# Head sums of half the sequence as accumulating transfers in place of matmuls, with 1 KB weight rows, four open output tiles and an early gate

## Chip, cores, metric

The kernel runs on one core of one Trainium2 chip. The metric is the device time of one execution in microseconds. Executions of one kernel mostly agree within 1%; each run below is four executions (one of them profiled) unless said otherwise, beside executions of the kernel before on the same chip.

## The reference, cut to what matters

Input x is 2048 x 512, everything bfloat16. The output mixes two branches with a gate per row.

```python
g = sigmoid((x * gate_w).sum(-1))                       # one number per row
# branch A: 32 heads of 16, each row attends to 8 rows, 0, 2, ..., 14 back
logits = einsum("bhsd,bhswd->bhsw", q, kg) * scale      # head sums: over d = 16
attn   = softmax(where(mask, logits, -1e9))
a      = einsum("bhsw,bhswd->bhsd", attn, vg) @ wo
# branch B: an MLP over the sequence axis
u = gelu(einsum("bsd,sf->bdf", layernorm(x), w1) + b1)  # f = 1792
y = einsum("bdf,fs->bds", u, w2) + b2
out = g * a + (1 - g) * y.transpose
```

## The kernel before: the parts that matter

The kernel is written as a list of operations with what each reads and writes; a small list scheduler in the kernel file orders them on each engine. `A("dve", ...)` puts one operation on an engine, `sch.dma("pool", ...)` issues a transfer from GpSimd (POOL). The sequence is treated in two halves `h`. TensorE (PE) does all matmuls; the vector engine (DVE) does the attention's products. Cuts are marked `# ...`.

```python
def f_sum(h, b0, with_gate):            # head sums on PE: 16 matmuls, 32 columns wide each
    # ... the 16 gate matmuls first if with_gate
        for wp in range(4):
            for c in range(4):
                ins = e.matmul(ps[32*c:32*c+32, 4+wp, :], lhsT=RP, rhs=sub(PB[b0], ...), tile_position=(0, 32*c))

for h in range(2):
    # ... q*k products of half h on DVE, in six buffers of 1 MB
    A("pe", f_sum(h, b0, h == 0), ..., name="sum%d" % h)
    A("act", act(LOG[h], ps[:, 4:8, :], AF.Copy), ..., name="lev%d" % h)     # logits leave PSUM
    A("dve", tt(M4, LOG[h][:, 0:4, :], LOG[h][:, 4:8, :], ALU.max), ...)     # softmax begins
    # ... max, subtract, exp, sums, 1/sum
    A("dve", tt(ATT[h], ATT[h], ..., ALU.mult), ..., name="nrm%d" % h)       # normalised weights
    for c in range(4):                  # spread them over the partitions: four copies of 512 KB
        prev = sch.dma("pool", ... e.dma_start(d_, s_) ..., name="av%d_%d" % (h, c))

AVD = (3, 4, 5)                         # attention products of 8 tiles; first add of these by DMA
def av_mult(u):
    AV(tt(pv, V5..., AVW[h]..., ALU.mult), 4.4, name="avm%d" % u)
    if u in AVD:
        sch.dma("pool", ... e.dma_start(o_, i_, accum_op=ALU.add) ..., name="avd%d" % u)   # 1 MB
def av_add4(u):
    if u not in AVD:
        AV(tt(pw(0, 4), pw(0, 4), pw(4, 4), ALU.add), 2.25, name="ava%d" % u)
def av_add(u):                          # two small adds, then the output projection may run
    AV(...1.19, name="avb%d" % u); AV(tt(OT[:, u], ...), 0.66, name="avc%d" % u)
```

Tile `u` needs copy `u % 4` of its half; the fifth product (`avm4`) is the first that needs a copy of half two. The three tiles whose big add is a transfer (3, 4, 5) are finished two products later.

## Time and profile before

| | before |
|---|---|
| time, median (range) | 165.43 us (165.14 to 165.48) |
| span of the profiled execution | 163.0 us |
| PE, DVE busy | 97%, 93% |
| softmax weights of half two normalised | 112.4 us |
| first of their copies issued; last landed | 112.70; 128.20 |
| first accumulating add issued; landed | 126.29; 134.11 |
| PE's last matmul ends | 159.54 |

How to read it: PE is busy nearly all of the span, so PE's own work sets the time, and DVE is close behind.

### The profile page before, as it was taken

The numbers are of one execution on the slowest core, as the hardware profiler recorded it, in microseconds if no ns is written. First come the engines' busy times: TensorE is split into PE (matmuls) and PEld (weight loads), VectorE is DVE, ScalarE is ACT, GpSimd is POOL, SyncE is SP. The second block draws the span as 40 slices with busy tenths as digits, with TensorE's granted clock in tenths as the row PEclk, the third lists the DMA queues.
The fourth block names the chain that finished last, engine by engine and source line by source line (L and its number), as shares of the span: only waits on it lengthen the run. The fifth ranks groups of instructions, "written<-read, shape, count | busy, mean of one in ns | idle before, by whom it ended". The sixth has DMA issues, their size and how long they took to land.

```text
span 163.0 us, 1989 instructions
## 1 busy us (share of the span) xinstructions
PE 158.6 (97%) x793; PEld 77.2 (47%) x808; DVE 151.1 (93%) x126; ACT 70.2 (43%) x100; POOL 12.0 (7%) x36
## 2 busy tenths in 40 slices
PE   7999999999999999999999999999999999999993
PEld 4855555555544344444444344444444444444641
DVE  1789999999999999999999999999999999999961
ACT  3367677666771579662111348011111111111164
POOL 3000030020000000023000000003100222000000
PEclk9999999999999999999999999999999999999999
DMA  5999979729499095999998976981997899991014
GB/s 165 311 268 259 221 183 263 140 38 191 101 277 292 24 242 157 261 290 290 303 245 233 260 188 177 290 209 30 300 243 193 186 207 193 205 216 36 32 59 134
DMA packets 44685, 32.24 MB, mean 198 GB/s; under 512 B 7941, under 2 KB 42245, under 8 KB 44677
## 3 DMA queue, kind: packets, MB, share of 16 engines
q1 hardware_dynamic: 41444, 22.06, 51.6%
q0 software_dynamic: 2512, 9.44, 27.3%
q10 hardware_dynamic: 720, 0.62, 1.2%
q8 instruction: 6, 0.10, 0.2%
q14 instruction: 3, 0.02, 0.0%
HBM read 18.88 MB, written 2.10 MB: 129 GB/s over the span
## 4 chain that ended last, share of the span: by engine, by line
PE 97%; ACT 1%; issue 1%
PE ps L858 30%; PE ps L885 30%; PE ps L649 23%; PE ps L894 8%; PE ps L588 2%; PE ps L551 2%; PE ps L722 1%; ACT arena L453 1%; PE ps L717 1%; PE ps L567 1%; PE ps L604 0%
## 5 line engine op out<-in xcount | busy, mean ns | idle before, releaser
L450 DVE TENSOR_TENSOR arena<-arena 128x4096 bf16<-128x4096 bf16 (+8 forms) x79 | 131.9, 1718 | 1.6 <-ACT arena L453 0.6
L885 PE MATMUL ps<-arena 128*128 128x512 bf16 (+2 forms) x234 | 50.0, 366 | 0.2
L858 PE MATMUL ps<-arena 128*128 128x512 bf16 x218 | 48.5, 379 | 0.3
L453 ACT ACTIVATE arena<-ps,arena 128x512 bf16<-128x512 f32 (+1 forms) x30 | 21.8, 731 | 60.7 <-PE ps L894 37.7
L453 ACT ACTIVATE arena<-ps 128x512 bf16<-128x512 f32 (+3 forms) x53 | 32.9, 629 | 17.4 <-PE ps L649 10.9
L649 PE MATMUL ps<-arena 128*128 128x512 bf16 x173 | 38.0, 379 | 0.2
L885 PEld LDWEIGHTS ps<-arena 128*128 128x128 bf16 x238 | 22.8, 98 | 25.9
L858 PEld LDWEIGHTS ps<-arena 128*128 128x128 bf16 x224 | 21.7, 98 | 26.8 <-issue 0.8
L649 PEld LDWEIGHTS ps<-arena 128*128 128x128 bf16 x176 | 19.9, 113 | 18.0
L894 PE MATMUL ps<-arena 128*128 128x512 bf16 (+2 forms) x67 | 15.6, 366 | 0.1
L453 ACT ACTIVATE arena<-arena 128x16 f32<-128x16 f32 (+5 forms) x10 | 6.7, 678 | 9.7 <-DVE arena L450 9.6
L954 ACT ACT_TABLE_LOAD x7 | 9.0, 1283 | 2.8 <-issue 2.7
L894 PEld LDWEIGHTS ps<-arena 128*128 128x128 bf16 x68 | 6.5, 98 | 7.3
L692 DVE BATCH_NORM_STATS2 arena<-arena 128x6 f32<-128x512 bf16 x16 | 9.9, 679 | 0.1
L790 POOL DMA_DIRECT2D arena<-arena x8 | 4.3, 560 | 75.1 <-DVE arena L450 75.1
L706 DVE TENSOR_SCALAR arena<-arena 128x512 bf16<-128x512 bf16 x16 | 5.3, 404 | 0.0
L827 POOL DMA_DIRECT2D arena<-arena x3 | 3.6, 1209 | 17.7 <-DVE arena L450 17.7
L747 POOL DMA_DIRECT2D arena<-arena x2 | 2.5, 1268 | 30.6 <-DVE arena L692 20.2
L579 DVE CAST arena<-ps 128x256 bf16<-128x256 f32 x4 | 1.6, 422 | 3.2 <-PE ps L567 3.2
L588 PE MATMUL ps<-arena 128*128 128x256 bf16 (+1 forms) x27 | 3.8, 284 | 0.2 <-ACT arena L453 0.2
L551 PE MATMUL ps<-const-bfloat16-1.0 128*128 128x512 bf16 (+1 forms) x9 | 2.7, 483 | 0.8 <-PEq L1004 0.8
L588 PEld LDWEIGHTS ps<-arena 128*128 128x128 bf16 x28 | 2.9, 113 | 0.7 <-DVE arena L579 0.4
(30 smaller groups left out, 14.4 us busy)
## 6 DMA issues: line engine op xcount, KB each, us to landing
arena<-in_B_w_dram SPq DMA_DIRECT2D x7, 1024.0 KB, 6.8
arena<-in_B_w_dram SPq DMA_DIRECT2D x8, 896.0 KB, 9.4
arena<-arena POOLq DMA_DIRECT2D x5, 1024.0 KB, 9.7
arena<-arena POOLq DMA_DIRECT2D x8, 512.0 KB, 11.2
out_dram<-arena SPq DMA_DIRECT2D x15, 128.0 KB, 3.1
arena<-in_A_x_dram SPq DMA_DIRECT2D x3, 512.0 KB, 4.7
arena<-in_A_wqkv_dram SPq DMA_DIRECT2D x2, 256.0 KB, 3.8
arena<-in_A_wqkv_dram SPq DMA_DIRECT2D x1, 512.0 KB, 5.6
```

Of the source, the lines that this page charges most:

```text
L450: return lambda e: e.tensor_tensor(out=o_, in0=a_, in1=b_, op=op_)
L453: return lambda e: e.activation(out=o_, in_=i_, func=f_, **kw)
L551: ins = e.matmul(ps[:, 7, 0:n_], lhsT=C1, rhs=nc.const_aps.tensor(1.0, (128, n_), BF16), start=True, stop=True)
L588: ins = e.matmul(ps[:, dl, c0:c1], lhsT=sub(WQKV, dt * 3 * D + dl, [(4, 128)]), rhs=XT[:, dt, c0:c1], start=(dt == 0 and hb == 0), stop=(d ...
L649: ins = e.matmul(ps[:, bank, :], lhsT=sub(WQKV, dt * 3 * D + tn * D + dl, [(4, 128)]), rhs=XT[:, dt, sb * 512:(sb + 1) * 512], start=(dt = ...
L692: A("dve", (lambda t_: lambda e: e.bn_stats(out=ST6[:, t_, :], in_=X[:, t_, :]))(t), 0.67, reads=["x%d" % t], writes=["st%d" % t], name="s ...
L706: A("dve", (lambda t_: lambda e: e.tensor_scalar(out=X[:, t_, :], in0=X[:, t_, :], scalar1=col(RSTD, t_), scalar2=col(NMR, t_), op0=ALU.mu ...
L790: prev = sch.dma("pool", (lambda d_, s_: lambda e: e.dma_start(d_, s_))(dst, src), 524288, sch.dsem("av%d_%d" % (h, c)), issue=1.0, reads= ...
L858: ins = e.matmul(ps[:, bank, :], lhsT=W1H[ft // 2][:, st, 128 * (ft % 2):128 * (ft % 2) + 128], rhs=X[:, st, :], start=(st == 0), stop=(st ...
L885: ins = e.matmul(ps[:, bank, 0:c1 - c0], lhsT=W2S[i // 2][:, ft, 128 * (i % 2):128 * (i % 2) + 128], rhs=UT[:, ft, c0:c1], start=(ft == 0) ...
L894: ins = e.matmul(ps[:, bank, 0:c1 - c0], lhsT=OT[:, i // 2, dl, 128 * (i % 2):128 * (i % 2) + 128], rhs=WO[:, dl, c0:c1], start=False, sto ...
L954: e.preload_act_table_set(want)
```

## The change

Its intent: take work from PE, the bound. The head sums of half two leave PE and are done by twelve transfers ("folds": four that add, four that move, four that move and add) on GpSimd's ring. Together they form the sum over four partitions that the matmuls formed. Weight loads get rows of 1 KB in place of 512 B, so the MLP works on four output tiles at a time; the gate's matmuls run early; eight of the 16 layer normalisations go to ScalarE (ACT); two of the W2 loads are held until the folds have landed. The core of the diff:

```diff
-            A("pe", f_sum(h, b0, h == 0), 1.2 + (1.0 if h == 0 else 0), ..., name="sum%d" % h, prio=-100, delay=0.2)
+            if h:
+                fas = {}
+                for s_ in range(2):
+                    for k_ in range(2):
+                        fas[s_] = fold("fa%d_%d%d" % (h, s_, k_), par(PB[b0], k_, ...), par(PB[b0], k_ + 2, ...), True, ...)
+                for s_ in range(2):
+                    for k_ in range(2):
+                        for c in (2 * s_, 2 * s_ + 1):
+                            fl = fold("%s%d_%d" % ("fb" if k_ == 0 else "fc", h, c), psub(LOG[h], 32 * c, ...), par(PB[b0], k_, ...), k_ == 1, ...,
+                                 after=[] if s_ else [fas[1]] if k_ else [avc_last[0]])
+                folds += [fas[1], fl]
+            else:
+                A("pe", f_sum(b0), 1.0, ..., name="sum%d" % h, prio=-100, delay=0.2)
 ...
-        W1H = [view(n_, BF16, [(256, NST), (1, 256)], ...
+        W1H = [view(n_, BF16, [(512, NST // 2), (1, 512)] if j_ else [(256, NST), (1, 256)], ...
 ...
-            ... load("w2_%d" % j, W2S[j], w2v[:, :, 256 * j:256 * j + 256], ...
+            ... load("w2_%d" % j, W2S[j], w2v[:, 7 * (j % 2):..., 512 * (j // 2):...], ..., deps={2: folds[0:1], 3: folds[1:2]}.get(j, []),
 ...
+            if t >= NST - 8:
+                A("act", act(X[:, t, :], X[:, t, :], AF.Identity, scale=col(RSTD, t), bias=col(NMR, t)), ..., name="ln%d" % t, prio=8)
+                continue
 ...
-            avlast[0] = A("dve", fn, dur, after=[avlast[0]] if avlast[0] else [], **kw)
+            avlast[0] = A("dve", fn, dur, after=([avlast[0]] if avlast[0] else []) + ([nrm[1]] if kw["name"] == "avm3" else []), **kw)
 ...
-        AVB = (2, 0, 1)
+        AVB = (2, 0, 2, 0, 1, 2, 0, 1)
```

The whole change also alters the scheduler's ties and its model of the transfers. The softmax of half two now stands behind the third attention product in DVE's order.

## The prediction

> **What bounds the kernel now.** I read the page first, then PE's waits, the chain that ended last, then the timelines of the vector engine (DVE) and of GpSimd (POOL), which issues the SBUF-to-SBUF transfers.
>
> ```profile
> PE 158.6 (97%) x793; PEld 77.2 (47%) x808; DVE 151.1 (93%) x126; ACT 70.2 (43%) x100; POOL 12.0 (7%) x36
> PE 97%; ACT 1%; issue 1%
> ```
>
> PE is busy for 97% of the 163.0 us span and is 97% of the chain. PE's waits, the whole answer:
>
> ```profile
> PE ps L551 <- PEq L1004: 0.8, 1, 0.8
> PE ps L588 <- ACT arena L453: 0.2, 1, 0.2
> ```
>
> So PE lost 1.0 us in all, at the start, and nothing in the middle. Only PE work taken away can shorten this kernel, and any new PE wait lengthens it. The pieces of the chain that matter (start, length):
>
> ```profile
> 53.70 0.98 PE ps L717 x16
> 54.68 0.86 PE ps L722 x16
> ...
> 91.91 0.98 PE ps L722 x16
> ...
> 155.19 4.33 PE ps L894 x20
> ```
>
> L717 is the gate, L722 the head sums (one per half of the sequence), L894 the output projection at the tail. A 512-column matmul of full size costs about 0.216 us (28 of them in 6.04 us of the L885 pieces); the 16 of a head sum take 0.9 us because four run side by side on 32 columns each.
>
> DVE is second with 93%, and its slack is small:
>
> ```profile
> 70.85 86.56 DVE L450 TENSOR_TENSOR arena<-arena 128x16 f32<-128x16 f32 x48
> 160.42 0.41 DVE L934 TENSOR_SCALAR arena<-ps,arena 128x128 bf16<-128x128 f32 x1 [3.01 <-PE ps L894]
> ```
>
> It runs without a gap to 70.85 + 86.56 = 157.41, where the last attention tile is ready. PE needs that tile for output tile 14, i.e. 0.86 + 0.65 + 0.22 = 1.73 us of L894 work before PE's end at 159.54, so at 157.81. The slack is 0.4 us. And the transfers behind it:
>
> ```profile
> 112.70 2.13 POOL L790 DMA_DIRECT2D arena<-arena  x4 [38.02 <-DVE arena L450]
> 126.29 1.22 POOL L827 DMA_DIRECT2D arena<-arena  x1 [11.46 <-DVE arena L450]
> 130.63 1.22 POOL L827 DMA_DIRECT2D arena<-arena  x1 [3.12 <-DVE arena L450]
> 134.95 1.19 POOL L827 DMA_DIRECT2D arena<-arena  x1 [3.11 <-DVE arena L450]
> ```
>
> L790 spreads the second half's softmax weights over the partitions (four copies of 512 KB, issued when DVE has normalised them, at about 112.3). L827 adds one half of a 2 MB product tile onto the other (accumulating, 1 MB each). Issue to landing, min/median/max, for these four copies and then for the three adds:
>
> ```profile
> DMA to landing us min/median/max: 7.8/10.7/13.9
> DMA to landing us min/median/max: 7.8/9.9/13.1
> ```
>
> The four copies land from 120.5 to 128.2 and the first add at 126.3 + 7.8 = 134.1. DVE wants that add's result at 134.57. So the normalised weights of half two must exist about 22 us before DVE wants the first add: that is the tight place.
>
> **What the Trainium skill says.** "DMA: Bandwidth & Descriptors", section "Issuing engines are not separate DMA queues": transfers issued from any engine run on the same 16 DMA engines and interleave. The trace agrees: from 112.7 to 134.1 the mean DMA share is 0.89, copies, adds, one W2 load and output stores together. The same page, "SWDGE vs HWDGE vs iDMA", says that accumulating must be issued from GpSimd, so the new folds go on the ring that already carries the copies and adds. "TensorE: Matmul & The Clock Gate", section "Part 3: Packing small matmuls", says tiles of 32 columns run concurrently; the 0.98 us for 16 agrees, so a head sum is cheap on PE.
>
> **The change part by part.**
> 1. Head sum of half two leaves PE: minus 0.86 to 0.98 us. Gate split off and moved into the projections: 16 matmuls before and after, zero on PE (it waits for DVE's copy of the gate weights at about 31.0; PE arrives at about 32.1).
> 2. Eight of 16 normalisations go from DVE to ACT. DVE spacing is 3.64 us for 11, less 0.08 of overlap, 0.325 each: minus 2.6 us, plus a 0.3 us wait for PE that goes. ACT pays about 8 x 0.67 = 5.4 us between 26 and 40, where it has 0.27 us idle beside each of some 20 evacuations (5.3 us). No PE wait expected, at most some tenths.
> 3. 1 KB rows: same bytes, half the packets. The packet records give 27 ns for 512 B and 46 ns for 1 KB, so 18% more per second. Weights are not late now, so no gain of itself. With four open tiles the loads are wanted in half-matrices; the two held W2 loads go out at about 92 and 101 and are wanted at 109 and 115: early enough by estimate.
> 4. Folds: four adds of 256 KB and eight moves of 128 KB on POOL's ring. DVE ends the products at about 86.8 (89.7 before, less 2.9); fold adds (about 4 us), moves (3), adding moves (3.5) and queueing end near 102. The softmax of half two now stands after the third product tile in DVE's order, at about 108, so DVE should not wait for the folds.
> 5. But that place is the cost. From 86.8 DVE runs three products (4.34 each), their adds, then the maxima, sums and so on. By the records: 30.9 us of DVE work, about 1.3 us for ACT's reciprocal (behind the eviction of output tile 0), 1.2 us for the normalisation: done at 120.2 instead of 112.3. The copies start 7.9 us later, while DVE has only three products (13.0 us) before it wants the first add, where it had 21.9 us.
>
> The first add's landing decides. DMA engine time after 120.5: 1.0 us start, W2's last load 896 x 46 ns / 16 = 2.6, copies 512 packets x 166 ns (the undisturbed packet) / 16 = 5.3, three stores 0.9, the add 256 x 350 ns / 16 = 5.6, landing 0.6: 136.5 if all engines are filled evenly. Scaled from before (21.4 us after the first copy's issue): 141.9, less 0.4 for the faster W2 load: 141.5. The copies ran at half of what the even case assumes both times before (last landing 15.5 us after the first issue), so I lean to 138.1. From the start of that addition DVE needs 22.84 us (157.41 - 134.57) and PE 1.79 more: PE's end = landing + 24.63 = 162.7, 3.2 us later than 159.54. Time: 165.45 + 3.2 = 168.6.
>
> **The rivals.**
> A. *PE stays the bound, nothing waits*: 165.45 - 0.9 = 164.6. It needs the add to land by 134.2, 13.7 us after the first copy's issue. For it: POOL's ring would be less disturbed if the 1 KB load is out of the way before the copies begin. Against: copies and add alone need 10.9 us of all engines plus start and landing.
> B. *Only the first copy's latency bites*: the fifth product wants it at 124.5; at 7.4 us it lands at 127.9, DVE waits 3.4, the additions start at 136.6, time 167.2.
> C. *The ring repeats the spacing of before*: landing 141.5, PE's end 166.1, time 172.0.
> D. *The folds are late as well*, because W2 loads and copies hold their ring: each us past 108 adds one; against it some 6 us of slack.
>
> **Range and chances.** 168.6 us; A below and C above give 164.6 to 172.2. Faster by over 2% (under 162.1) is more than the removed PE work can give: 0.02. The limit of slower is 168.8, about the centre; with A and B on one side: same 0.46, slower 0.52.
>
> **What would show it.** Right: PE's first wait in its tail, at the output projection of tile 6 (about 137), some 3 to 4 us, released by DVE; DVE idle some 3 us before the fifth product and again before the addition after the sixth, released by transfers of L832 and L870 (the new lines of copies and adds); the normalised weights at about 120; no PE wait before 115; head sums of 16 on PE once only. Wrong: DVE without idle time after 120 and PE's end near 158.7 (rival A: the copies land twice as fast as before); or DVE waiting at about 108 for the folds (rival D); or PE waiting for banks between 26 and 42 (ACT overloaded by the normalisations) or for a W2 load at 109 or 115.

## More of the kernel before

The busy tenths of the page, in 40 slices of 4.1 us each:

```profile
PE   7999999999999999999999999999999999999993
PEclk9999999999999999999999999999999999999999
DMA  5999979729499095999998976981997899991014
```

The first row is PE's busy share, the second the clock it was granted, the third the share of the 16 DMA engines: in slices 29 to 36, from 114 to 147 us, they are near their limit while copies, adds, a weight load and stores run.

## The result, and the profile after

The changed kernel takes 179.04 us (178.03 to 180.2), the kernel before 165.43: a ratio of 1.0829, 95% interval 1.076 to 1.0897. Ratios here are the mean time of one kernel's fast runs over that of the other's of the same rounds, so not quite the ratio of the medians quoted. Executions over 1.5% slower than the fastest of the same kernel are left out of the means. All outputs are right. The profiled execution (180.2) is the longest of its four, with a span of 178.2 us; its event times carry about 1 us of that.

First the page of the changed kernel, the same rows as before:

```profile
PE 161.5 (91%) x777; PEld 77.7 (44%) x792; DVE 149.1 (84%) x118; ACT 72.2 (41%) x107; POOL 21.4 (12%) x48
PE   7999999999999999999999999999999002999994
PEclk9999999999999999999999999999999955599999
DMA  5999979787995953999987779926999999520004
DVE 52%; DMA 17%; PE 14%; issue 7%; SPq 7%; ACT 2%; DVEq 0%
```

PE has a hole of over two slices from 138 us on, and its granted clock is about half of full speed in three slices, late in the hole and just after it. The last row is the chain that ended last: it was 97% PE and now runs through DVE and a DMA. The whole answer on PE's waits (line, releaser: total us, times, longest):

```profile
PE ps L943 <- DVE arena L452: 12.2, 1, 12.2
PE ps L554 <- PEq L1059: 0.8, 1, 0.8
```

One wait, of 12.2 us, at L943, the output projection. DVE waited as well:

```profile
DVE arena L452 <- DMA arena<-arena: 13.9, 2, 8.6
```

13.9 us in two pieces for a transfer, where the kernel before had none. The chain says which transfer (start, length, what):

```profile
125.81 22.36 DMA arena<-arena
148.16 0.02 issue
148.19 1.24 DVE arena L452
149.42 0.02 issue
149.44 0.70 DVE arena L452
150.15 0.05 issue
150.19 1.89 PE ps L943 x4
```

One accumulating add, issued at 125.81, landed 22.36 us later; two small additions of DVE follow it, and then PE goes on. In GpSimd's timeline (start, length, engine, line, operation, in brackets what ended its idle time before) it is the first line of L870, behind the four copies of L832:

```profile
121.48 2.21 POOL L832 DMA_DIRECT2D arena<-arena  x4 [18.28 <-DVE arena L452]
125.81 1.24 POOL L870 DMA_DIRECT2D arena<-arena  x1 [2.12 <-DVE arena L452]
135.56 1.22 POOL L870 DMA_DIRECT2D arena<-arena  x1 [8.52 <-DVE arena L452]
139.89 1.19 POOL L870 DMA_DIRECT2D arena<-arena  x1 [3.11 <-DVE arena L452]
```

The copies go out 8.8 us later than before (112.70), but the first add is asked for at the same moment as before (126.29). Issue to landing, for L832 and then for L870:

```profile
DMA to landing us min/median/max: 9.3/13.5/19.3
DMA to landing us min/median/max: 18.0/18.9/22.4
```

The last copy needs 19.3 us (13.9 before) and the adds 18.0 to 22.4 (7.8 to 13.1 before). DVE's timeline shows both waits, 5.33 us for the first copy and 8.59 for the first add:

```profile
119.95 5.56 DVE L452 TENSOR_TENSOR arena<-arena 128x2048 bf16<-128x2048 bf16 x2 [0.52 <-ACT arena L455]
130.83 8.76 DVE L452 TENSOR_TENSOR arena<-arena 128x8192 bf16<-128x8192 bf16 x2 [5.33 <-DMA arena<-arena]
148.19 22.84 DVE L452 TENSOR_TENSOR arena<-arena 128x2048 bf16<-128x2048 bf16 x14 [8.59 <-DMA arena<-arena]
```

And PE's timeline shows a second loss behind the first, in the pieces after the wait:

```profile
136.33 1.67 PE L934 MATMUL ps<-arena 128*128 128x512 bf16 x7
150.19 1.89 PE L943 MATMUL ps<-arena 128*128 128x512 bf16 x4 [12.19 <-DVE arena L452]
151.88 3.19 PE L934 MATMUL ps<-arena 128*128 128x512 bf16 x7
154.86 1.67 PE L943 MATMUL ps<-arena 128*128 128x512 bf16 x4
```

Seven matmuls that took 1.67 us just before the wait take 3.19 just after it; four take 1.89 and then 1.67 where they otherwise take 1.03. That is 1.52 + 0.86 + 0.64 = 3.0 us. PE's last matmul ends at 174.71, 15.2 us later than in the profile of before: 12.2 of wait and 3.0 of slow clock. The 0.9 us of the removed head sum do not show in this difference, because PE was 0.75 us behind from the start in this execution: its clock rose to full speed at 5.96 us (4.27 before), so that its long run of projection matmuls began at 9.34 us (8.59 before).

The packet records of GpSimd's ring tell why the add is so late. From the first copy's issue to the first add's landing they hold 3072 KB in the kernel before, just the four copies and that add, at 294 ns for a 4 KB packet on average. In the changed kernel they hold 3936 KB: 864 KB of the second and third add had been moved as well, at 339 ns a packet, and all packets together took 26.4 us of each engine's time in 26.7 us (19.2 of 21.4 before). So the engines were full, and part of what filled them was work that nobody was waiting for.

The semaphore records tell how that could be. Each transfer reports sixteen completions, as many as there are DMA engines. Those of the first add come from 138.8 to 148.2 us in the changed kernel, a spread of 9.4 us, and from 133.8 to 134.1 in the kernel before. Those of the last copy come from 133.2 to 142.4, and from 123.0 to 128.2 before. So the engines were out of step, and as far as the numbers tell (no record names a packet's engine) the add landed when the last of them was through with its copies and then with its share of the add. The Trainium skill, "DMA: Bandwidth & Descriptors", section "Two DMAs through the same engine are not ordered", says that nothing orders transfers across the 16 engines; the spread fits that. The 864 KB are what the others moved meanwhile: the sixteen completions average 143.6, 4.6 us before the last, and 864 KB at 339 ns for 4 KB are an estimated 864 / 4 x 339 ns / 16 = 4.6 us of each engine.

### The profile page after: what moved, and what is told of

Same layout as the page of the kernel before. It is cut to its first block, busy times and chain, and to the rows that moved or that the text cites. A ratio compares the mean times of both kernels' runs of the same rounds, so it can differ in the third digit from the quotient of the medians.

```text
span 178.2 us, 1970 instructions
## 1 busy us (share of the span) xinstructions
PE 161.5 (91%) x777; PEld 77.7 (44%) x792; DVE 149.1 (84%) x118; ACT 72.2 (41%) x107; POOL 21.4 (12%) x48
## 4 chain that ended last, share of the span: by engine, by line
DVE 52%; DMA 17%; PE 14%; issue 7%; SPq 7%; ACT 2%; DVEq 0%
DVE arena L452 48%; DMA arena<-arena 13%; PE ps L934 8%; SPq L495 6%; PE ps L943 5%; DMA arena<-in_A_x_dram 4%; ACT arena L455 2%; DVE arena L713 2%; DVE arena L695 1%; SPq L496 1%; DVE arena L847 0%; DVE arena L685 0%; DVE arena L706 0%; DVE arena L702 0%; DVE arena L845 0%
## 5 line engine op out<-in xcount | busy, mean ns | idle before, releaser
L452 DVE TENSOR_TENSOR arena<-arena 128x4096 bf16<-128x4096 bf16 (+7 forms) x79 | 132.7, 1719 | 16.2 <-DMA arena<-arena 13.9
L934 PE MATMUL ps<-arena 128*128 128x512 bf16 (+2 forms) x236 | 51.6, 374 | 0.1
L455 ACT ACTIVATE arena<-ps 128x512 bf16<-128x512 f32 (+3 forms) x52 | 30.8, 603 | 14.5 <-PE ps L652 6.3
L934 PEld LDWEIGHTS ps<-arena 128*128 128x128 bf16 x238 | 23.1, 99 | 27.3 <-issue 2.2
L902 PEld LDWEIGHTS ps<-arena 128*128 128x128 bf16 x224 | 21.8, 98 | 26.6 <-issue 0.4
L943 PE MATMUL ps<-arena 128*128 128x512 bf16 (+2 forms) x64 | 16.6, 393 | 12.4 <-DVE arena L452 12.2
L652 PEld LDWEIGHTS ps<-arena 128*128 128x128 bf16 x176 | 19.8, 113 | 18.2 <-ACT arena L455 0.4
L455 ACT ACTIVATE arena<-arena 128x512 bf16<-128x512 bf16 (+6 forms) x18 | 13.2, 733 | 22.1 <-DVE arena L452 22.1
L791 POOL DMA_DIRECT2D arena<-arena x12 | 9.3, 880 | 56.9 <-DVE arena L452 48.9
L943 PEld LDWEIGHTS ps<-arena 128*128 128x128 bf16 x68 | 6.8, 103 | 20.6 <-DVE arena L452 12.7
L832 POOL DMA_DIRECT2D arena<-arena x8 | 4.4, 572 | 19.9 <-DVE arena L452 19.9
L763 POOL DMA_DIRECT2D arena<-arena x2 | 2.5, 1266 | 28.5 <-DVE arena L695 21.5
L870 POOL DMA_DIRECT2D arena<-arena x3 | 3.6, 1215 | 13.7 <-DVE arena L452 13.7
L591 PE MATMUL ps<-arena 128*128 128x256 bf16 (+1 forms) x27 | 4.4, 313 | 0.2
L591 PEld LDWEIGHTS ps<-arena 128*128 128x128 bf16 x28 | 3.1, 120 | 1.1 <-DVE arena L582 0.4
```

Of the source, the lines that this page charges most:

```text
L452: return lambda e: e.tensor_tensor(out=o_, in0=a_, in1=b_, op=op_)
L455: return lambda e: e.activation(out=o_, in_=i_, func=f_, **kw)
L591: ins = e.matmul(ps[:, dl, c0:c1], lhsT=sub(WQKV, dt * 3 * D + dl, [(4, 128)]), rhs=XT[:, dt, c0:c1], start=(dt == 0 and hb == 0), stop=(d ...
L652: ins = e.matmul(ps[:, bank, :], lhsT=sub(WQKV, dt * 3 * D + tn * D + dl, [(4, 128)]), rhs=XT[:, dt, sb * 512:(sb + 1) * 512], start=(dt = ...
L791: return sch.dma("pool", lambda e: e.dma_start(o_, i_, **kw), nb, sch.dsem(name), issue=1.1, reads=reads, writes=writes, name=name, after= ...
L832: prev = sch.dma("pool", (lambda d_, s_: lambda e: e.dma_start(d_, s_))(dst, src), 524288, sch.dsem("av%d_%d" % (h, c)), issue=1.0, reads= ...
```

## The experiments

Theories ahead of the runs: (1) *the late normalisation* costs the time, folds or not; (2) *the folds' traffic or the held loads* cost it; (3) *something else in the change* (four open tiles, 1 KB rows, normalisations on ACT) costs it; and inside (1), whether the ring shared by copies and adds or the DMA engines as such make the add late. "Changed" means the changed kernel. The small diffs are against it unless said otherwise.

### e1_pesum: the change without its folds

```diff
-            if h:
+            if h and not PESUM:      # PESUM = True: half two takes the PE branch too; no folds, nothing held behind them
-            bank = (0, 1, 2, 3, 0, 1, 4, 5, 6, 7, 2, 3, 0, 1)[ft]
+            bank = (0, 1, 2, 3, 0, 1, 2, 3, 0, 1, 2, 3, 0, 1)[ft]   # banks 4 to 7 hold the sums again
```

> The changed kernel with the head sums of the second half back on the tensor engine (no folds, no held W2 loads; the MLP's banks 4 to 7 replaced by 2, 3, 0, 1 because the head sum needs them). Theory 1 (the late normalisation makes the copies meet the adds): normalised weights at 110 to 113, first add lands by 135, no wait of PE over 1 us, time 164.5 to 166.5. Theory 2 (the traffic of the folds slows the ring): the same, 164.5 to 166.5. Theory 3 (something else of the change, as 1 KB rows, four open tiles, normalisations on ACT or the order of the tail): over 170.

Measured: 165.73 us, before 165.74; ratio 1.0011 (0.9972 to 1.005). PE has no wait but the one at the start. The copies go out at 109.91, and the first add lands at 132.73. So all other parts of the change together are neutral: theory 3 falls.

### e2_pesum_late: no folds, but the softmax as late as in the change

```diff
  # e1_pesum, and:
+        mx4[1].order.add([o for o in sch.ops if o.name == "avm2"][0])   # maxima of half two after the third product
```

> As e1_pesum, but the softmax of the second half may start only after the third product tile on DVE, as in the changed kernel: the lateness without any fold. Theory 1: normalised weights at 120 to 121.5, copies land 9 to 19 us after the first issue, first add at 144 to 149, PE waits 8 to 13 us at the output projection of tile 6, time 175 to 181. Theory 2: no fold traffic, so copies as before, first add at 136 to 140, time 166 to 170.

Measured: 176.35 us, before 165.74 at the same rounds; ratio 1.0617 (1.0549 to 1.0685). PE's first wait is the changed kernel's, without one fold in the kernel:

```profile
PE ps L947 <- DVE arena L453: 9.2, 1, 9.2
```

Copies at 121.38, the first add asked for at 125.72 and landed at 146.47. 10.6 of the 13.6 us come from the place of the softmax alone. Theory 1 stands. For the other 3 us there is only the difference of the two profiles: here the add lands 1.7 us sooner, and the slow clock behind the wait costs 1.9 us in place of 3.0.

### e3_dummy and e9_dummynohold: the folds as traffic only

Both have the sum on PE and send all twelve folds as well, into a buffer that is only read as a dependence; e9_dummynohold leaves out the holding back of the two W2 loads.

```diff
  # e3_dummy: half two takes the PE sum, then sends the folds, issued after it
-                            fl = fold(..., psub(LOG[h], 32 * c, ...), ..., ["log%d_%d" % (h, c)], ...
+                            fl = fold(..., psub(OUTS, 32 * c, ...), ..., ["fo%d" % c], ...
  # e9_dummynohold, besides:
-               ..., order=False, deps={2: folds[0:1], 3: folds[1:2]}.get(j, []),
+               ..., order=False,
```

> As e1_pesum (head sum on PE is the one that is used, softmax early), but all twelve folds are sent as well, after the head sum, into the unused output buffer, with the two W2 loads held behind them: the traffic without the lateness. Theory 1: normalised weights at 110 to 113, time 165 to 168. Theory 2: copies and adds pushed back by the folds, DVE waits over 5 us, time 172 or more.

Measured: 175.46 us, ratio 1.0603 (1.0552 to 1.0654), which looks like theory 2. But the page says otherwise:

```profile
PE ps L936 <- ACT arena L455: 7.5, 1, 7.5
```

PE waits for ACT, not for DVE, and at 142.6 rather than 138. ACT had no free output buffer, because the stores of the outputs stood behind the held W2 loads on SyncE's queue: the last two loads were issued at 108.33 and 116.14 and landed at 135.25 and 148.89, and the first stores behind them at 149.2 to 150.3. Five W2 loads went out between 106.3 and 116.1, just ahead of and beside the four copies (110.1 on). The dummy folds start only after the sum and end later than the real ones (last landing 113.7 against 106.0). That is a fault of the experiment, and the next one takes the hold away.

> As e3_dummy (head sum on PE, softmax early, folds sent as unused traffic), but the two W2 loads are not held behind the folds. In e3_dummy the copies landed as in e1_pesum and PE waited for stores stuck behind late W2 loads. If the held loads were its whole cost: W2 landed by 115, no PE wait over 2 us, time 165 to 167.5. If the traffic of the folds itself costs: 170 or more.

Measured: 165.84 us, ratio 1.0023 (1.0008 to 1.0038). The folds' own traffic costs about 0.4 us (0.6 at the upper end of the interval). The last six W2 loads were issued from 84.1 to 109.4, and had all landed by 129.1. What e3_dummy lost was the hold. Theory 2 falls for the traffic where the softmax is early. The traffic is not without effect: the first add landed 25.9 us after the first copy's issue, against 22.8 in e1_pesum, and the early start hid it. The hold is dangerous, but in the changed kernel PE waited for no W2 load.

### e4_early: the softmax of half two as soon as the folds land

```diff
+        [o for o in sch.ops if o.name == "avm2"][0].order.add(nrm[1])    # third product only after the normalisation
```

> The changed kernel, but the third product tile must wait for the normalisation, so the softmax of the second half comes right after the folds land (106). Theory 1: normalised weights at 116 to 117.5, first add at 136 to 141, PE waits 1 to 5 us, time 167 to 172. Theory 2: the folds still go, first add as late as in the changed kernel, time 176 or more.

Measured: 172.92 us, ratio 1.0439 (1.0367 to 1.051). The folds landed at 107.85, DVE idled 2.9 us for them and about 3 us for ACT's exponential and logarithm; the copies went out at 118.01, the first add landed at 141.68, PE waited 5.7 us. An earlier softmax helps by 6.1 us, but the folds themselves are too late to give back the rest. The wait, the landing and the time all lie just beyond the range of theory 1.

### e5_w2held: the last W2 load out of the copies' way

```diff
-deps={2: folds[0:1], 3: folds[1:2]}
+deps={2: folds[0:1], 3: folds[1:2], 7: [the last copy of half two]}
```

> The changed kernel, but the last W2 load (896 KB, otherwise issued together with the copies of the second half) must wait until all four copies have landed. If that load's head start is what delays the copies: first copy lands 7 us after its issue instead of 9.3, first add 3 us earlier (near 145), time 175 to 177. If only the meeting of copies and adds matters: within 1 us of the changed kernel, 178 to 180.

Measured: 177.77 us, ratio 1.0742 (1.0708 to 1.0777); first add landed at 146.86, PE's wait 10.6 us. The load that shares the engines with the copies costs little over 1 us: a small term, in the right direction, and between the two forecasts.

### e6_dveadds and e14_twoadds: which adds go on the ring

```diff
-        AVD = (3, 4, 5)
+        AVD = ()          # e6_dveadds: all three on DVE
+        AVD = (4, 5)      # e14_twoadds: only the first one on DVE
```

> The changed kernel, but the three additions that accumulating transfers make are made on DVE (2.2 us each), so the ring carries the four copies alone after 121. If the adds on the ring slow the copies and are what DVE waits for: copies land within 15.5 us as in the kernel before, the wait at tile 6 goes, DVE's chain ends near 164.8, PE waits some 7 us at tile 14, time 169 to 173. If the ring is slow for another reason, the last copy still lands 19 us after the first issue and the time is over 175.

Measured: 172.88 us, ratio 1.0436 (1.0404 to 1.0468). With no add beside them the four copies took 17.1 us from first issue to last landing (20.9 in the changed kernel). DVE hardly waits any more, but its 156.1 us of work end at 165.15, and PE waits for it at the very end:

```profile
165.20 3.59 PE L943 MATMUL ps<-arena 128*128 128x512 bf16 x12 [6.41 <-DVE arena L452]
```

> The changed kernel with the first of the three adds (fourth product) on the vector engine, the other two still as accumulating transfers. The vector engine was idle for 5.3 us after the fourth product, waiting for the first copy, and the add with its two small ones is some 4.2 us of its work, so it should fit there. Theory 'the end is set by the first add's landing': tile 6 is ready near 130, PE does not wait at 138, the vector engine loses about 1 us before the fifth product and at most 2 to 3 before the next addition, and ends near 161 to 163; time 167 to 170. Rival 'every add on the ring is late by as much': the second add takes the place of the first, it lands near 150, PE waits about as long at tile 8, time 175 or more.

Measured: 167.62 us, ratio 1.0128 (1.0095 to 1.016); the one profiled execution was a slow one (170.15) and is left out of the ratio. Moving 2.3 us of work onto DVE gains 11.4 us. DVE's timeline from there, in that slow execution:

```profile
120.35 9.87 DVE L452 TENSOR_TENSOR arena<-arena 128x2048 bf16<-128x2048 bf16 x5 [0.52 <-ACT arena L455]
130.50 13.10 DVE L452 TENSOR_TENSOR arena<-arena 128x8192 bf16<-128x8192 bf16 x3 [0.28 <-DMA arena<-arena]
145.50 16.52 DVE L452 TENSOR_TENSOR arena<-arena 128x2048 bf16<-128x2048 bf16 x11 [1.90 <-DMA arena<-arena]
```

The add and its two small ones fill the time in which DVE had waited for the first copy (5.33 us, now 0.28), and the first add that is still a transfer is asked for at 135.22, when the copies are nearly through: it lands 10.3 us later, not 22.4, and DVE waits 1.9 us. PE still waits 3.6 us, at 143.9, for output tile 8, the first that needs the next attention tile, and loses 1.4 us more to half clock behind it. How long it waits in the fast executions is not known: their mean clock is 0.999 to 1.0 (0.990 in the slow one), so there the half clock did not come.

### e7_addsheld: no add is asked for before the copies have landed

```diff
-                        sch.dsem("avd%d" % u), issue=1.3, writes=res, name="avd%d" % u)
+                        sch.dsem("avd%d" % u), issue=1.3, writes=res, name="avd%d" % u, deps=[the last copy of half two])
```

> The changed kernel with one wait more: the three accumulating adds are issued only when the last copy of half two has landed. In the changed kernel the four copies took 20.9 us from the first issue to the last landing beside the adds' packets, and 17.1 us in the run whose adds were on the vector engine. Theory 'copies and adds slow each other on the one ring': the copies land in about 16 to 17 us again, near 138, the first add is issued then and lands in the 7.8 us of the kernel before, near 146; the time is 1 to 3 us better, 176 to 178. Rival 'the engines do the same sum of work in either order': the add's start and landing latency comes on top, it lands near 150 or later, and the time is 180 or more.

Measured: 178.92 us, ratio 1.0806 (1.0742 to 1.0869), so level with the changed kernel. The copies landed by 138.72 (17.3 us) and the first add, issued at 139.29, at 147.22: both as the first theory wanted, but the add comes only 0.9 us sooner than when it was asked for 13.5 us earlier, and the third lands at 158.41 against 158.79. The time lies between the two forecasts. Read: held back, the add leaves the engines in step (its sixteen completions come within 0.2 us) and lets the copies land 3.7 us sooner, but it lands 8.5 us after the last copy in place of 5.8. So asking early and asking late come to nearly the same here.

### e8_copiesact: the copies of half two from ACT's queue

```diff
-                prev = sch.dma("pool", ...
+                prev = sch.dma("act" if h else "pool", ..., prio=-40 if h else 0, ...
```

> The changed kernel, but ACT issues the four copies of the second half, on its own hardware queue, so copies and adds are no longer on one ring. If the shared ring[...] is the limit: first add lands by 138 and the time falls to 168 to 172. If the 16 engines are the limit, whoever issues: first add at 144 or later, time 175 to 181.

Measured: 174.7 us, ratio 1.056 (1.054 to 1.058). The copies were no faster (22.3 us from first issue to last landing, the last one issued 2.7 us later than in the changed kernel), as the section on issuing engines that the prediction names has it. But the add, alone on its ring, no longer lands about 6 us after the last copy but 0.6 us after it, at 143.98. PE waits 5.7 us for it, and 2.1 us more earlier, for an eviction by ACT, which took up to 3.4 us to issue a copy. So a ring of its own gains the add 4.2 us; the second forecast, of the engines as the limit, is nearly met (144 or later, 175 or more).

### e10_act0early and e15_filled: how much of the loss comes back

In e4_early the folds still queued behind the copies of *half one* on the ring. e10_act0early sends those from ACT; e15_filled puts two small additions of the second product into the time in which DVE waits for ACT's exponential.

```diff
  # e10_act0early: e4_early, and
-                prev = sch.dma("pool", ...
+                prev = sch.dma("pool" if h else "act", ..., prio=0 if h else -40, ...
  # e15_filled: e10_act0early, and
+        [o for o in sch.ops if o.name == "avb1"][0].order.add([o for o in sch.ops if o.name == "msub1"][0])
```

> The early-softmax kernel (softmax of half two before the third product; 172.9 us) with, besides, the four copies of half one issued from ScalarE's queue, so that the folds of half two no longer queue behind them on GpSimd's ring (there the copies landed as late as 93.3 and the folds of the second projection half, issued at 88.7, took 9 to 10 us). Theory 'it is the ring position of the folds that makes the softmax late': the last fold lands near 103 in place of 107.9, the normalised weights are ready near 113 to 114, the first add lands near 137, PE waits 1 to 2 us, the time is 166 to 169. Rival 'the DMA engines are the limit, whatever queue': the folds land within 1.5 us of before and the time stays 171 to 174.

Measured: 168.18 us, ratio 1.0169 (1.011 to 1.0228). The last fold landed at 103.45 (107.85 in e4_early), the copies went out at 115.04, the first add landed at 138.05, and PE's wait was:

```profile
PE ps L945 <- DVE arena L452: 2.0, 1, 2.0
```

After 2.0 us of idle time PE's clock did not drop: the four matmuls behind it took 1.04 us. (This is the fastest of the four executions; two of the others have a mean clock of 0.99.)

> The kernel with early softmax and half one's copies on ScalarE's queue (168.2 us), with two small additions of the second product tile (1.9 us together) moved into the 2.0 us for which the vector engine waits for ScalarE's exponential. Theory 'what is left of the loss is how late the first add is asked for and lands': the normalised weights are ready 1 to 1.9 us sooner, near 112 to 112.6, the first add lands near 136.5, PE waits under 1 us in its tail, the time is 165.5 to 167, level with the kernel before or 1% slower; below 165 it would beat both. Rival: the folds are then what the maxima wait for, so that only half of it is gained, and the time stays at 167.5 or more.

Measured in five rounds: 166.56 us, before 165.72; ratio 1.0043 (1.0001 to 1.0084), without the one slow execution of six (169.09). Copies at 114.39, only 0.65 us sooner than in e10_act0early: DVE came 1.1 us later to the first attention product in this execution (88.84 against 87.71), and the filling itself gained 1.8 us from there on. Add landed at 137.50, PE's wait in the tail 0.3 us. With the path repaired the folds are level with the matmuls that they replace, or a little slower; no version beat the kernel before.

### The runs side by side

Times in us from the span's start, from the transfers' issue and landing records.

| kernel | first copy issued | last copy landed | first add asked | first add landed | landed after first copy's issue | PE waits for DVE |
|---|---|---|---|---|---|---|
| before | 112.70 | 128.20 | 126.29 | 134.11 | 21.4 | 0 |
| e1_pesum | 109.91 | 125.49 | 124.77 | 132.73 | 22.8 | 0 |
| e15_filled | 114.39 | 131.28 | 127.37 | 137.50 | 23.1 | 0.3 |
| e10_act0early | 115.04 | 131.91 | 128.02 | 138.05 | 23.0 | 2.0 |
| e14_twoadds (slow execution) | 121.88 | 139.26 | 135.22 | 145.47 | 23.6 | 3.6 |
| e4_early | 118.01 | 135.67 | 130.99 | 141.68 | 23.7 | 5.7 |
| e2_pesum_late | 121.38 | 140.71 | 125.72 | 146.47 | 25.1 | 9.2 |
| e5_w2held | 121.52 | 141.35 | 125.84 | 146.86 | 25.3 | 10.6 |
| changed | 121.48 | 142.38 | 125.81 | 148.16 | 26.7 | 12.2 |

In all of these copies and adds share GpSimd's ring, and the add lands 5.5 to 7.2 us after the last copy, whenever it was asked for. That is about what one engine needs for its share of the add, an estimated 16 packets x 339 ns = 5.4 us. Where it was asked for some 13 to 15 us after the first copy, the whole takes 21.4 to 23.7 us; where it was asked for 4.3 us after it, 25.1 to 26.7. The two dummy runs, which are not in the table, do not follow this: asked for 14.8 us after the first copy, their adds landed 25.9 us (e9_dummynohold) and 26.6 us (e3_dummy) after it, with W2 loads under way beside the copies.

## Why the prediction was wrong, step by step

The mechanism and its place were right; its size was not. That it would be slower was given hardly more than an even chance (0.52).

- *Step 1, the head sum leaves PE*: 16 fewer matmuls, as predicted. e1_pesum and e15_filled show how little there was to win: both are level with the kernel before.
- *Step 2, normalisations on ACT*: no wait of PE between 26 and 42. Right. *Step 3, 1 KB rows and held loads*: no wait for a weight in the changed kernel. Right, though the held loads went out at 98.9 and 105.1, not at 92 and 101; e3_dummy shows that the hold has little room. (Two slips: 27 and 46 ns a packet make 17% more, not 18%, and the range ends at 172.2 where rival C gives 172.0.)
- *Step 4, the folds*: landed at 106.0, not "near 102", and the maxima, at 109.98, did not wait. The slack of 6 us was 4. Of the 4 us 1.6 come from DVE, which ended the products at 88.4, not 86.8. e4_early and e10_act0early show what they queued behind: the copies of half one, worth 4.4 us of the last landing.
- *Step 5, the late place*: normalised at 121.2 (predicted 120.2). PE's first wait in its tail at tile 6, at 138.0 (predicted "about 137"), released by DVE, which in turn waits before the fifth product and again before the addition after the sixth. In place and releaser all as predicted, and none of the signs listed under "Wrong" came; the sizes were not (waits of 5.3 and 8.6 us of DVE for "some 3", 12.2 us of PE for "3 to 4"). e2_pesum_late confirms the cause with no fold in the kernel.
- *The term that failed is the first add's landing*: predicted 138.1, measured 148.16. Even the ring-repeats rival, at 141.5, was 6.7 us short. In the even case the engines are through with the copies 9.8 us after the first issue (1.0 + 2.6 + 5.3 + 0.9), and the add takes 6.2 us more. The runs have 17.1 to 17.3 us for the copies with no add beside them (e6_dveadds, e7_addsheld) and 20.9 us with the adds asked for early (changed); the add landed 5.8 us after them, so the add itself was priced well. Against the even case's 136.5 that is 7.4 + 3.7 - 0.4 us, and 1.0 us because the first copy went out later than forecast: the whole 11.7 us. Two assumptions made the copies too cheap. A packet was priced at 166 ns, 5.3 us of each engine: about two thirds of the packets on the ring in the kernel before, from 112.7 to 128.2, are that short (under 175 ns), but their mean is 261 ns, and e7_addsheld has 282 ns, 9.05 us of each engine. And the engines were taken as evenly filled, while in the changed kernel they ended the last copy from 133.2 to 142.4. The prediction knew the 15.5 us of the kernel before and let them count for only 1.6 us, by leaning from 136.5 to 138.1, for which it shows no sum.
- *A term that the sum lacked*: PE after an idle time. The Trainium skill, "TensorE: Matmul & The Clock Gate", section "Part 1: The HAM clock gate", says that PE falls to half clock after an idle window of about 3.4 us and comes back after a busy one. The runs agree: 2.0 us of waiting cost nothing more, and behind waits of 5.7 to 12.2 us the half clock was granted for 6.8, 10.2 or 13.65 us, which are multiples of 3.41. That cost 1.7 us (e8_copiesact, e3_dummy) to 3.0 us (changed), and not in the order of the waits: 5.7 us cost 2.8 us in e4_early. (e6_dveadds, whose wait has only twelve matmuls behind it, is left out.) I had looked up the page for the head sums and not for what a wait does.
- *The sum again, with measured terms*: PE's end was predicted as landing + 24.63 = 162.7. Measured: 148.16 + 26.55 = 174.71. Of the 12.0 us between them 10.1 are the landing and 1.9 a longer way from the landing to the end, in which the slow clock's 3.0 us lie. That way is another than predicted: not 22.84 us of DVE and 1.79 of PE, but 2 us of DVE and then PE alone. In device time the miss is 10.4 us (179.04 against 168.6); most of the other 1.6 us comes from setting the profile of one execution, the slowest, against medians.

Not separated: why the copies need 17 us and not 10 by themselves, and why adds asked for early put the engines so far out of step. The rise from 294 to 339 ns a packet is in part only the mix, since an add's packet is longer than a copy's (357 against 299 ns in e8_copiesact, where they have separate queues) and more of them fall into the longer stretch.

## What to carry to other kernels

When a change moves a transfer's start nearer to its use, price the whole queue with the mean packet time that the same transfers show in their crowded stretch (282 ns here, not 166), and look at when the last of the 16 engines is through: in the changed kernel the add landed 4.6 us after the mean of its sixteen completions. A transfer that is asked for early does not land early for that; here it landed 5.5 to 7.2 us after the last copy either way. Work that a waiting engine could do itself belongs there: one add of 2.3 us put into a wait of 5.3 us was worth 11.4 us. Before taking 0.9 us from the bounding engine, look at where the scheduler puts what depended on it; here waits of PE of 5.7 us and more also cost 1.7 to 3.0 us of half clock.

## What the Trainium skill lacked or had wrong

- "DMA: Bandwidth & Descriptors" gives no cost for accumulating SBUF-to-SBUF packets beside copies: here 294 ns for a 4 KB packet of copies and one add, 339 ns with three adds queued, while about two thirds of the copies' packets in the kernel before took 159 to 175 ns.
- I found in no page a number for how far the 16 engines drift apart under such a queue: the sixteen completions of one add spread over 9.4 us in the changed kernel, 0.3 us in the kernel before and 0.2 us where the add was held back.
- "DMA: Bandwidth & Descriptors", section "Issuing engines are not separate DMA queues", says that issuing from several engines saves sequencer time only. Read alone, that falls short here: the copies indeed were no faster from ACT's queue (22.3 us), but the add, now alone on its ring, landed 4.2 us sooner (143.98 against 148.16), although the last copy landed 1.0 us later. And issuing took ACT up to 3.4 us.
- "TensorE: Matmul & The Clock Gate", Part 1, calls the ramp under 1% of a typical span. It says this of the cold matmuls at a kernel's start, and nothing here contradicts it; one wait in the tail cost 3.0 us of half clock besides, 1.7% of the 178.2 us span. The window that it states agrees with the runs.
